# Clearing one table row later, reordering the first transfers and preparing fewer weight pieces in the first attention of an attention and FNet kernel

## The chip, the cores and the metric

The kernel runs on one core of one Trainium2 chip. The metric is the device time of that core in microseconds (us), as the median of several executions. In the text PE is TensorE, DVE is VectorE, ACT is ScalarE, POOL is GpSimd, and SP is SyncE, whose queue issues nearly all transfers (DMA). The granted clock is the share of TensorE's full clock that the profiler records as allowed: in the changed kernel the S matmuls of a tile took 0.70 us at 1.00 (at 167.63 us) and 1.14 at 0.50 (at 178.10). I call 0.50 the half clock.

## The reference

```python
# q, k, v: (8 batches, 8 heads, 576 positions, 64), float32
# attention inside chunks of 64 positions
s = scale * q_c @ k_c.T;  p = softmax(s);  x = p @ v_c      # -> (8, 576, 512)
# FNet block, per batch
u  = x + Re(FFT over channels(FFT over positions(x)))
un = (u - mean) / sqrt(var + 1e-6)
out = u + relu(un @ w_ch1) @ w_ch2         # 512 -> 2048 -> 512
```

The two weights come in as float64. The kernel turns them into float32 on the chip.

## The kernel before

A tile is two chunks of 64 positions with all heads, and 36 tiles make the eight batches. Tiles 0 to 4 are batch 0 (tile 0 also holds a chunk of batch 1). The attention of a batch yields steps. For tile n these are **S** (scores), **T** of the next tile (transposes of q and k), **V** of the tile before (P·V), and **P** (transpose of the exponentials). Batch 0 has 20 steps, 0 to 19.

```python
def att_T(n):                                   # cut
    pt = turn(lambda j: a[:, 2 * j:2 * j + 2, :].rearrange("p h d -> p (h d)"))   # PE transposes
    nc.scalar.copy(t[:, :, CH:0:-1] if low else t[:, :, 0:CH], ...)
    if low:
        nc.gpsimd.tensor_copy(t[:, :, 0:1], t[:, :, CH:CH + 1])    # GpSimd's query copy
    ...                                         # the same for k, its copy on VectorE

def load_tables():                              # start: sequence tables (cut)
    nc.sync.dma_start(out=cd, in_=dim_tab[:, 0:2, 0:HM + 1])
    nc.sync.dma_start(out=cs[:, HM + 1:DM], in_=dim_tab[:, 2, 1:HM])
    nc.sync.dma_start(out=sd, in_=dim_tab[:, 3, 1:HM])
    nc.gpsimd.memset(cs[:, 0:HM + 1], 0.0)
    nc.sync.dma_start(out=cs[0:1, 0:HM + 1], in_=dim_tab[0:1, 2, 0:HM + 1])
    nc.gpsimd.memset(cs[0:1, HM + 1:DM], 0.0)   # waits for the transfer into cs

def round_weight(i):                            # one round: front half of piece i, back half of i-1
    nc.vector.tensor_scalar(wi, hi, 0x000FFFFF, ...)          # VectorE
    nc.scalar.activation(out=w, ...)                          # ScalarE, three times (cut)
    nc.vector.tensor_scalar(p, hi, 0x7FF00000, ...)           # VectorE
    nc.vector.scalar_tensor_tensor(w, lo, ...)                # VectorE, of piece i-1
    nc.vector.scalar_tensor_tensor(p, hi, ...)                # VectorE
    nc.gpsimd.tensor_tensor(out=w, in0=w, in1=p, op=ALU.mult) # GpSimd
    load_weight(max(raws, default=i - 1) + 1)   # a freed buffer fetches the next piece, 512 KB

def shift(b):    # after V(2): one row each of the low tiles goes to the next tile
    ...          # gather by DMA into "first", then scatter by DMA back, on SP's queue
```

After the shift, the fold adds and subtracts low and high tiles on VectorE and gives `pm`. The Fourier stage is two sets of matmuls, z (over positions, from `pm`) and mix (over channels). Then follow the norms and the MLP in groups of tiles, with matmuls up and dn. In group 0 of the MLP one or two rounds are issued per step until all 33 are done. The attention of batch 1 starts between the dn matmuls of that group:

```python
t0 = KF + 1 if cur == 0 else ...                # KF = 16 steps of "up" first
```

The start of the driver issues the transfers, and the loop of batch 0 has the rounds at steps 4, 7, 10, 13, 16 and 19:

```python
for n in range(first[1]):                       # q, k of tiles 0 to 4, v of 0 to 2,
    load(n)                                     # three weight pieces after tile 1,
    ...                                         # the tables after tile 2 (cut)
for i in range(3, len(RAWS)):
    load_weight(i)
for step, _ in enumerate(attention(0)):
    if step == 9:
        turn_tables()
    if step > 3 and step % 3 == 1:
        round_next()
for step, _ in enumerate(fourier(0)):
    if step < 4:
        round_next()
    ...
```

## Time and profile before

| | before |
|---|---|
| median of 3 executions | 1332.5 us (1331.69 to 1332.6) |
| span in the profile | 1332.0 us (that execution took 1333.76) |
| PE busy | 1265.9 us, 95% |
| S of tile 1 starts | 29.14 us |
| gather of the shift issued | 53.97 us |
| z runs without a gap from | 62.83 us |
| MLP starts (first up matmul) | 97.63 us |
| dn of group 0 starts | 166.56 us |
| first S of batch 1 | 173.52 us |
| up of group 1 starts | 265.11 us |

The lower rows are read from the timeline. They are the landmarks by which two kernels are compared. Before the change 36 of PE's 66 us of idle time lie in the first 63 us and another 17 between there and dn. From 265 us on it is busy for 1058.9 of 1067 us, so a microsecond saved early should reach the end unless something in between eats it.

The view of waits sums, for PE in the first 60 us, what ended its idle time. Its columns are the total in us, how often, and the longest. The row at its top is the one that the change is aimed at:

```profile
PE sc L269 <- POOL qT L254: 14.6, 1, 14.6
```

### The profile page before, as it was taken

What the parts mean: (1) busy time and instruction counts of PE and PEld (TensorE: products, weight loads), DVE (VectorE), ACT (ScalarE), POOL (GpSimd) and SP (SyncE); (2) the same over time, 40 slices, a digit from 0 to 9 for tenths busy, and PEclk for the clock granted to TensorE, in tenths of its full rate; (3) what the DMA queues carried; (4) which work ended last, traced back from release to release, by engine and by line L of the source; (5) the groups of instructions that cost most, each with busy time, mean ns of one, the idle gap of its engine ahead of it and who ended that gap; (6) DMA issues with size and microseconds to landing.
All of it is one profiled execution on the core that took longest, in us unless ns stands there. A gap on an engine that the chain in (4) does not pass through costs nothing.

```text
span 1332.0 us, 13660 instructions
## 1 busy us (share of the span) xinstructions
PE 1265.9 (95%) x5616; PEld 611.1 (46%) x5616; DVE 345.4 (26%) x649; ACT 253.4 (19%) x517; POOL 124.9 (9%) x186
## 2 busy tenths in 40 slices
PE   3679798999999999999999999999999999999998
PEld 2434354544444445544444445444444444444443
DVE  1868951511132104210322033211411130001000
ACT  1537720122011201121112111210111001100100
POOL 0214402101100201002100210020002010000000
PEclk9669998999999999999999999999999999999999
DMA  9734431122012101211021002210100000000000
GB/s 194 170 91 142 142 73 41 25 56 48 16 32 51 37 7 26 57 31 33 16 56 40 17 15 48 50 41 8 32 17 1 8 16 8 0 16 16 0 8 24
DMA packets 126260, 56.99 MB, mean 43 GB/s; under 512 B 116533, under 2 KB 117046, under 8 KB 126198
## 3 DMA queue, kind: packets, MB, share of 16 engines
q1 hardware_dynamic: 124598, 55.73, 17.0%
q8 instruction: 44, 0.72, 0.2%
q10 hardware_dynamic: 1600, 0.39, 0.2%
q14 instruction: 18, 0.15, 0.0%
HBM read 46.50 MB, written 9.44 MB: 42 GB/s over the span
## 4 chain that ended last, share of the span: by engine, by line
PE 88%; DVE 5%; DMA 2%; SPq 2%; ACT 1%; issue 1%; POOL 1%; DVEq 0%; ACTq 0%; POOLq 0%
PE dn L553 37%; PE up L541 34%; PE z L418 5%; PE pt L242 4%; PE mix L461 4%; PE sc L269 1%; PE xp L307 1%; PE z L428 1%; DVE power L223 1%; DMA xall<-in_moe_w_ch_dram 1%; SPq L156 1%; DVE power L231 1%; DVE w L221 1%; DVE w L230 1%; DVE unT L510 1%
## 5 line engine op out<-in xcount | busy, mean ns | idle before, releaser
L541 PE MATMUL up<-unT,w 128*128 128x512 f32 x1152 | 518.2, 601 | 9.1 <-ACT h L548 8.2
L553 PE MATMUL dn<-w,h 128*128 128x512 f32 x1152 | 517.5, 599 | 0.0
L541 PEld LDWEIGHTS up<-unT,w 128*128 128x128 f32 x1152 | 213.8, 191 | 255.9 <-issue 239.7
L553 PEld LDWEIGHTS dn<-w,h 128*128 128x128 f32 x1152 | 213.5, 191 | 246.0 <-issue 243.6
L548 ACT ACTIVATE h<-up 128x512 f32<-128x512 f32 x144 | 85.7, 595 | 427.1 <-PE up L541 427.0
L572 DVE TENSOR_TENSOR o<-dn,xall 128x512 f32<-128x512 f32 x36 | 24.8, 690 | 248.6 <-PE dn L553 248.6
L278 DVE TENSOR_REDUCE mx<-sc 128x8 f32<-128x512 f32 x36 | 24.8, 690 | 221.8 <-PE sc L269 221.8
L316 DVE TENSOR_TENSOR xall<-xp,rd 128x512 f32<-128x512 f32 x36 | 24.8, 689 | 127.0 <-PE xp L307 127.0
L232 POOL TENSOR_TENSOR w<-w,power 128x512 f32<-128x512 f32 x32 | 43.4, 1357 | 88.9 <-DVE power L231 88.9
L418 PE MATMUL z<-tk,pm 128*128 128x289 f32 x128 | 42.5, 456 | 7.2 <-POOL pm L362 4.0
L476 POOL TENSOR_TENSOR xall<-y,xall 128x513 f32<-128x513 f32 x14 | 24.2, 1727 | 258.7 <-DVE y L469 258.7
L286 ACT ACTIVATE ex<-ex 128x512 f32<-128x512 f32 x36 | 22.6, 629 | 107.1 <-DVE ex L280 107.1
L269 PE MATMUL sc<-kT,qT 64*64 64x64 f32 x1152 | 26.8, 235 | 16.1 <-POOL qT L254 14.6
L436 ACT COPY zf<-z 128x256 f32<-128x256 f32 x32 | 11.9, 372 | 149.1 <-PE z L418 103.8
L269 PEld LDWEIGHTS sc<-kT,qT 64*64 64x64 f32 x1152 | 21.7, 143 | 37.7 <-issue 21.9
L418 PEld LDWEIGHTS z<-tk,pm 128*128 128x128 f32 x128 | 25.7, 208 | 27.9 <-issue 16.3
L259 DVE COPY kT<-pt 128x512 f32<-128x512 f32 x36 | 24.5, 681 | 48.1 <-PE pt L242 48.1
L307 PEld LDWEIGHTS xp<-v,pT 64*64 64x64 f32 x1152 | 21.2, 141 | 26.7 <-issue 22.2
L512 ACT COPY unT<-pt 128x512 f32<-128x512 f32 x18 | 10.5, 584 | 111.6 <-PE pt L242 111.6
L254 POOL COPY qT<-qT 128x8 f32<-128x8 f32 x16 | 3.2, 199 | 300.9 <-ACT qT L252 300.9
L288 DVE TENSOR_REDUCE rd<-ex 128x8 f32<-128x512 f32 x36 | 24.7, 686 | 25.8 <-ACT ex L286 25.8
L242 PEld LDWEIGHTS pt<-ident,un 128*128 128x128 f32 x144 | 18.6, 147 | 25.8 <-issue 22.2
(87 smaller groups left out, 762.7 us busy)
## 6 DMA issues: line engine op xcount, KB each, us to landing
xall<-in_moe_w_ch_dram SPq DMA_DIRECT2D x32, 512.0 KB
v<-in_v_dram SPq DMA_DIRECT2D x142, 64.0 KB
q<-in_q_dram SPq DMA_DIRECT2D x34, 128.0 KB
k<-in_k_dram SPq DMA_DIRECT2D x34, 128.0 KB
out_dram<-o SPq DMA_DIRECT2D x16, 256.0 KB
out_dram<-o SPq DMA_DIRECT2D x32, 128.0 KB
q<-in_q_dram SPq DMA_DIRECT2D x14, 256.0 KB
k<-in_k_dram SPq DMA_DIRECT2D x14, 256.0 KB
```

Of the source, the lines that this page charges most:

```text
L232: nc.gpsimd.tensor_tensor(out=w, in0=w, in1=p.bitcast(FP32), op=ALU.mult)
L242: nc.tensor.transpose(pt[:, j, :], src(j), ident)
L269: nc.tensor.matmul(out=sc[t0:t0 + CH, e, j * CH:(j + 1) * CH], lhsT=a[r0:r0 + D, 2 * j + c, 0:CH], rhs=b[r0:r0 + D, j, t0:t0 + CH], start= ...
L278: nc.vector.tensor_reduce(out=mx, in_=s4, axis=AX.X, op=ALU.max)
L307: nc.tensor.matmul(out=xp[t0:t0 + CH, e, j * D:(j + 1) * D], lhsT=a[r0:r0 + CH, j, t0:t0 + CH], rhs=b[r0:r0 + CH, c, j, :], start=True, st ...
L316: nc.vector.tensor_tensor(out=xo.rearrange("p (j e d) -> p e j d", j=NJ, e=2), in0=xp[:, :, 0:NJ * D].rearrange("p e (j d) -> p e j d", j=NJ),
L418: nc.tensor.matmul(out=z[:, 0:NQ], lhsT=pm[p, fold_, half], rhs=tk[p, i, fold_, :], start=(i == 0), stop=(i == NM), skip_group_check=(T == 2),
L461: nc.tensor.matmul(out=o[:, cols], lhsT=zt[:, T], rhs=tab, start=(T == 0), stop=(T == 3), skip_group_check=True,)
L541: nc.tensor.matmul(out=up[:, 0:cols], lhsT=w1[:, kk, m * 128:(m + 1) * 128], rhs=unT[:, kk, 0:cols], start=(kk == 0), stop=(kk == KD - 1),)
L548: nc.scalar.activation(out=h1[:, m, 0:cols], in_=up[:, 0:cols], func=ACTF.Relu)
L553: nc.tensor.matmul(out=dn, lhsT=h1[:, m, s * 128:(s + 1) * 128], rhs=w2[:, m, :], start=(m == 0), stop=(m == KF - 1),)
L572: nc.vector.tensor_tensor(out=o, in0=dn, in1=natural(n), op=ALU.add)
```

## The change

The change takes the clearing of one row of the table `cs` off the way of GpSimd's query copy. It orders the first transfers by when they are needed. It does three of six rounds later, outside the attention, and it puts the addition of high tiles (the HI add) on GpSimd for batch 0 too.

```diff
@@ load_tables
             nc.sync.dma_start(out=t[r0 + 1:r0 + CH, NM], in_=seq_tab[1:CH, NM])
+
+    def load_dim_tables():
         nc.sync.dma_start(out=cd, in_=dim_tab[:, 0:2, 0:HM + 1])
         ...
         nc.sync.dma_start(out=cs[0:1, 0:HM + 1], in_=dim_tab[0:1, 2, 0:HM + 1])
-        nc.gpsimd.memset(cs[0:1, HM + 1:DM], 0.0)
@@ turn_tables, called at step 9
         nc.scalar.copy(a[:, :, NL + 1:NQ], b[:, :, NL + 1:NQ])
+        nc.gpsimd.memset(cs[0:1, HM + 1:DM], 0.0)
@@ fourier
-                eng = nc.gpsimd if kind(n) == HI and b > 0 else nc.vector
+                eng = nc.gpsimd if kind(n) == HI else nc.vector
@@ driver
-        for n in range(first[1]):
+        for n in range(3):
             load(n)
-            if n < 3:
-                load_v(n)
-            if n == 1:
-                for i in range(3):
-                    load_weight(i)
-            if n == 2:
-                load_tables()
-        for i in range(3, len(RAWS)):
+            load_v(n)
+        load(3)
+        load_tables()
+        load_weight(0)
+        load(4)
+        load_weight(1)
+        load_dim_tables()
+        for i in range(2, len(RAWS)):
             load_weight(i)
@@ attention of batch 0
-            if step > 3 and step % 3 == 1:
+            if step > 7 and step % 4 == 1:
                 round_next()
```

The last line makes the steps 9, 13 and 17. In the changed kernel the line numbers are two higher (L269 becomes L271, and so on).

## The prediction

> **What bounds the kernel now.** I read the page first, then the waits and the timeline of the first 210 us, the DMA view of the first 40 us, and the busy time by stretch. The page's slices are 33.3 us each.
>
> ```profile
> PE   3679798999999999999999999999999999999998
> ...
> PEclk9669998999999999999999999999999999999999
> DMA  9734431122012101211021002210100000000000
> ```
>
> TensorE (PE) is the bound from the fourth slice on. The change acts on the first five: the first batch's attention and Fourier stage, while there is no other batch to fill PE. Of 66 us in which PE is idle (1332.0 span less 1265.9 busy), most lies there. The largest single idle time is 14.62 us:
>
> ```profile
> 28.64 0.30 POOL L179 MEMSET cs<- 1x255 f32 x1 [27.08 <-DMA cs<-in_dim_tab_dram]
> 28.89 0.19 POOL L254 COPY qT<-qT 128x8 f32<-128x8 f32 x1
> ...
> 29.14 1.13 PE L269 MATMUL sc<-kT,qT 64*64 64x64 f32 x32 [14.62 <-POOL qT L254]
> ```
>
> GpSimd (POOL) stands at the clearing of one row of cs until a table transfer lands; the small copy of tile 1's queries is behind it, and PE behind that copy. The data of tile 1 had long been there. But DMA is at nine tenths or more in this slice too (0.90 to 1.00 in each 10 us up to 40, by the busy times of stretches). The DMA view of 0 to 40 us, one column per us:
>
> ```profile
> GB/s 0 0 142 194 195 164 186 215 216 182 151 235 205 328 397 355 293 171 99 113 103 213 222 194 147 235 310 226 155 178 181 180 197 199 281 341 330 150 27 14
> DMA packets 16599, 7.72 MB, mean 193 GB/s; under 512 B 15061, under 2 KB 15574, under 8 KB 16598
> ```
>
> q, k and v come in 256 B packets at 180 to 200 GB/s (columns 3 to 7 and 29 to 33), the weight pieces (4 KB packets) at 330 to 400. All that is issued ahead of the loop lands by about 37 us.
>
> The end of the first attention is not bound by PE either:
>
> ```profile
> 53.97 1.22 SPq L334 DMA_DIRECT2D first<-xall  x2
> ...
> 57.16 1.14 PE L307 MATMUL xp<-v,pT 64*64 64x64 f32 x32 [2.35 <-ACT pT L297]
> ...
> 58.05 0.69 DVE L351 TENSOR_TENSOR sum<-xall 128x512 f32<-128x512 f32 x1 [1.31 <-DMA xall<-first]
> ...
> 62.83 1.33 PE L418 MATMUL z<-tk,pm 128*128 128x289 f32 x2 [1.71 <-DVE pm L362]
> ```
>
> The rows' shift (L334, the transfer queue SP issues it) is a gather and a scatter by DMA; the fold waits for it, and the Fourier matmuls for the fold. PE runs densely from 62.83.
>
> Then the first MLP group, where 23 of the 33 rounds of weight preparation are done:
>
> ```profile
> 97.60:166.60 69.00, 60.74 (x129) 25.71 (x130) 61.36 (x85) 48.74 (x78) 29.07 (x21) 0.94 0.42 137
> ```
>
> Columns: stretch, length, busy us of PE, PE loads, VectorE (DVE), ScalarE (ACT), POOL. DVE is the bound there (61.4 of 69): 128 up matmuls at 0.43 us would be 55 us, and PE waits 8.2 us for h, which queues on ACT between the rounds.
>
> **What the Trainium skill says.** "TensorE: Matmul & The Clock Gate", table at its head: VectorE, ScalarE and GpSimdE have strict first-in first-out queues. The trace agrees: a ready 0.19 us copy stood 14 us behind a memset. "GPSIMD Engine Reference", Engine selection: two-input elementwise work is about twice as slow there as on VectorE. The trace: the HI add takes 1.727 us on POOL and 0.66 us on DVE, 2.6 times. "DMA: Bandwidth & Descriptors", Specifications: line rate wants 512 B or more. Agrees: 187 GB/s in 2 to 10 us, all 256 B, against 330 to 400 for weights. The first page, Part 1, says about 3.4 us of sustained work releases the half clock. The trace differs: the z matmuls are back to back from 62.8 to 82.5 and that stretch's mean granted clock is 0.50.
>
> **The change part by part.**
>
> *Clearing the row later.* The copy follows its query copy, so tile 1's scores start when kT is out, at 13.95 + 0.64 = 14.6 instead of 29.1. That is 14.5 us for PE, at first. New bound: transfers.
>
> *Order of transfers.* In MB: q, k, v of tiles 0 to 2 2.36; q, k of 3 0.52; sequence table 0.89; w0 0.52; q, k of 4 0.52; w1 0.52; dimension tables 0.53; w2 to w4 1.57. Tiles 0 to 2 at 187 GB/s take 12.6 us and land at some 15 us, in time. Tile 4's q and k land near 26, needed near 27. The total, 7.4 MB, is the same, so all of it still lands at 36 to 37. Behind it, in SP's order and ahead of the gather, are v3 0.26, q5 k5 0.52, v4 0.26, q6 k6 0.52, v5 0.26. Before, v3 landed at 38 and two weight pieces (w5, w6) stood among the rest; now there are none. 1.57 MB at 185 GB/s is 8.5 us: v5 lands at 36.5..38 + 8.5 = 45 to 46.5. Before, the gather was issued 1.5 us ahead of v5's landing (53.97), so now at 43.7 to 45: earlier by 9 to 10, not 14.5. So transfers cut the 14.5 us by a third.
>
> *Fewer pieces.* Rounds at attention steps 9, 13, 17 instead of 4, 7, 10, 13, 16, 19. A round costs DVE 0.42 + 0.42 + 0.68 + 0.68 = 2.2 us and ACT 0.63 + 0.71 + 0.72 = 2.06. Three fewer would spare 6.6 us of DVE, but attention now waits for DMA, so this hides nothing more. And step 17 is a bad place: it comes after the folds, which wait for the shift, and ahead of tile 4's pT copy. That copy on ACT then waits for the fold, L221 0.42, ACT's three 2.06; then follow pT 0.58, V matmuls 1.1, the product 0.7, POOL 0.3, sum 0.7, pm 0.4: z about 6.4 us after the last fold (60.67 before), where it was 62.83 - 60.67 = 2.2. That gives back 4.2. z starts densely at about 44.4 + (60.67 - 53.97) + 6.4 = 57.5, or 57 if DMA has fewer holes: 5.5 us earlier.
>
> *HI add on POOL.* y is ready, DVE does LO's add 0.69 and statistics 0.69 + 0.18, POOL the HI add 1.5 to 1.7 meanwhile. DVE's 0.66 goes, a wait of 0.2 to 0.3 comes: 0.4 us, twice: 0.8. The MLP starts 6.3 us earlier, at 91.3.
>
> *The three rounds that moved.* In the MLP they run at (170.6 - 97.4) / 23 = 3.18 us each, 3.05 without the slow start: 9.2 us more of DVE. Up's pace, 1.5 rounds a step, does not change. But the last two are issued after h of m = 15, ahead of batch 1's scores:
>
> ```profile
> 170.68 1.26 POOL L232 TENSOR_TENSOR w<-w,power 128x512 f32<-128x512 f32 x1 [0.63 <-DVE power L231]
> ...
> 174.28 0.69 DVE L278 TENSOR_REDUCE mx<-sc 128x8 f32<-128x512 f32 x1 [3.68 <-PE sc L269]
> ...
> 178.51 0.60 PE L242 MATMUL pt<-ident,ex 128*128 128x128 f32 x4
> 179.04 0.69 PE L269 MATMUL sc<-kT,qT 64*64 64x64 f32 x32
> ```
>
> DVE has 3.68 us of slack at mx; 9.2 more makes it late by 5.5. PE has dn matmuls until 178.5, 1.4 us after what P needs. I expect P and the next scores 3.4 to 4.9 us later: 4 us lost. w2's last pieces come in time (needed some 85 us after the MLP's start, done at 83).
>
> Sum: 5.5 + 0.8 - 4 = 2.3 us off 1332.5, so 1330. The two losses (step 17 and DVE's lateness) are derived from program order and could be smaller; DMA could also have fewer holes than before (99 to 113 GB/s at 18 to 20 us). I put 1328.
>
> **Rivals.** (a) The wait goes and nothing takes its place: 14.5 + 6.6 + 0.8 = 22 us, 1310. For it: the wait is single and large. Against it: DMA's nine tenths in the first slice. (b) Clock: a denser attention keeps PE at full clock and z's 19.7 us at 0.50 become some 12: 8 us below the figure above, 1320. Against it: PE still has to wait for the shift right ahead of z. (c) The moved rounds cost their whole 9.2 us, or a pause in dn lets the clock fall: 9.2 - 4 = 5.2 us worse than the sum, 1335.5. For it: DVE is the bound in that stage.
>
> **Range and chances.** 1316 to 1336 holds half of (b), and nearly all of (c). Faster by 2% needs 26.6 us, more than (a): 0.02. Slower by 2%: 0.01. Within: 0.97.
>
> **What would show it.** Right: no wait of PE for the query copy; tile 1's scores near 14.7 us; DMA at 9 tenths without a gap to some 45 us; the gather at 44 to 45; the fold's wait for the scatter longer than 1.31; round 2 between fold and V of tile 4; z dense from 57; the MLP from 91; mx of batch 1 late, PE idle 3 to 5 us before its P. Wrong if the gather comes well before 43, if z starts before 54, or if dn shows no new idle time. After that stage all should be equal, shifted.

## The result

| | before | changed |
|---|---|---|
| median | 1332.1 us (1329.53 to 1332.6, 4 executions) | 1335.12 us (1334.33 to 1335.66, 4 executions) |
| span in the profile | 1332.0 | 1332.5 |
| S of tile 1 | 29.14 | 14.72 |
| gather issued | 53.97 | 46.37 |
| last fold operation ahead of tile 4's product ends | 60.67 | 52.69 |
| z without a gap from | 62.83 | 59.44 |
| MLP | 97.63 | 93.57 |
| dn of group 0 | 166.56 | 160.67 |
| first S of batch 1 | 173.52 | 167.63 |
| second S of batch 1 | 179.04 | 178.10 |
| up of group 1 | 265.11 | 265.63 |

The ratio is 1.0026, with a 95% interval of 1.0009 to 1.0043. Here and below a ratio is the mean time of one kernel's fast executions over the mean of the other's in the same rounds of timing, so it is not quite the ratio of the medians quoted. The change lies within 2%. A second timing of the changed kernel, on another chip, gave 1.0010 (0.9998 to 1.0022). So no gain is shown. The change probably costs a few us: 3.5 and 1.3 by the two ratios, 3.0 and 2.3 by the medians; only the first interval excludes zero. The two profiled spans differ by only 0.5 us. The profiled execution of before was slower than its median (1333.76 against 1332.1) and that of the changed kernel a little faster (1334.33 against 1335.12), so the two profiles explain where time was moved but understate the loss.

The page of the changed kernel, in its 40 slices of 33.3 us (tenths of busy time, granted clock, DMA's share):

```profile
PE   5479888999999999999999999999999999999998
...
PEclk8569988999999999999999999999999999999999
DMA  9625431022012101211021002210100000000000
```

The first slice of PE went from 3 to 5, the second from 6 to 4. The wait has moved one slice to the right. DMA's first digit is still 9, and the sixth slice (167 to 200 us) fell from 9 to 8 for PE and to 8 for the clock.

The waits of PE in the first 60 us (total, times, longest):

```profile
PE xp L309 <- ACT pT L299: 10.4, 1, 10.4
PE pt L244 <- DMA start<-in_q_dram: 6.8, 1, 6.8
PE pt L244 <- DMA q<-in_q_dram: 6.1, 1, 6.1
PE pt L244 <- DMA cs<-in_dim_tab_dram: 3.3, 1, 3.3
```

The row for the query copy is gone. In its place stand waits for transfers of 6.1 and 3.3 us, and a new largest one: 10.4 us in front of V of tile 4. (The profile puts the 3.3 us down to a transfer into `cs`. What these transposes read is tile 4's q, and in e2 the same wait is booked to q.) The timeline of the changed kernel shows what holds the gather. Its columns are start, length, engine, operation, and in brackets the idle time before it and what ended that:

```profile
14.72 1.14 PE L271 MATMUL sc<-kT,qT 64*64 64x64 f32 x32 [0.22 <-DVE kT L261]
...
32.66 0.69 DVE L318 TENSOR_TENSOR xall<-xp,rd 128x512 f32<-128x512 f32 x1 [0.40 <-PE xp L309]
...
35.56 2.98 SPq L146 DMA_DIRECT2D k<-in_k_dram  x1
...
40.81 1.09 PE L244 MATMUL pt<-ident,q 128*128 128x128 f32 x4 [6.11 <-DMA q<-in_q_dram]
```

Tile 1's scores start 14.42 us earlier, as intended. But SP spends 2.98 us on the issue of one k transfer, while the weight pieces and tables issued ahead of it drain (the last piece lands at 38.13). From 31.52 to 46.37 us SP does nothing but issue seven groups of q, k and v (2.59, 1.36, 2.98, 2.69, 0.60, 0.58 and 3.56 us, together 14.36 of 14.85), and the gather is next in that queue. What it copies was ready long before: tile 2's product (L318) ends at 33.35 us, 13.0 us ahead of the gather. In the kernel before, that product ended at 48.69, 5.3 us ahead. So the data came 15.34 us earlier, and the gather only 7.60.

The timeline around the shift and the round of step 17:

```profile
46.37 1.21 SPq L336 DMA_DIRECT2D first<-xall  x2
...
50.47 0.69 DVE L353 TENSOR_TENSOR sum<-xall 128x512 f32<-128x512 f32 x1 [5.57 <-DMA xall<-first]
...
52.62 0.41 DVE L223 TENSOR_SCALAR w<-xall 128x512 uint32<-128x512 uint32 x1
...
54.96 0.57 ACT L299 COPY pT<-pt 128x512 f32<-128x512 f32 x1
...
55.58 1.13 PE L309 MATMUL xp<-v,pT 64*64 64x64 f32 x32 [10.40 <-ACT pT L299]
...
59.44 1.33 PE L420 MATMUL z<-tk,pm 128*128 128x289 f32 x2 [1.46 <-DVE pm L364]
```

DVE waits 5.57 us for the scatter and folds. Then it begins the round (52.62), on whose ACT instructions tile 4's pT copy has to wait in ACT's queue. That copy runs at 54.96. P·V of tile 4, the product, the last fold and z are behind it. The gather came 7.60 us earlier than before, z only 3.39.

The second place is the start of batch 1 in the first MLP group, in the same view:

```profile
172.50 1.75 DVE L233 SCALAR_TENSOR_TENSOR power<-xall,power 128x512 uint32<-128x512 uint32 x1
174.17 0.68 DVE L280 TENSOR_REDUCE mx<-sc 128x8 f32<-128x512 f32 x1
...
176.76 1.12 PE L244 MATMUL pt<-ident,ex 128*128 128x128 f32 x4 [3.98 <-ACT qT L254]
...
178.10 1.14 PE L271 MATMUL sc<-kT,qT 64*64 64x64 f32 x32 [0.22 <-DVE kT L261]
```

The scores had been ready since about 168.3 us, but DVE was still on the rounds that the change had moved here. PE stands still for 3.98 us. Before, there was no such pause. The stretch view (length, busy us of PE, PE loads, DVE, ACT, POOL, then the granted clock, DMA's share, GB/s) shows what followed in the changed kernel:

```profile
172.80:182.00 9.20, 5.02 (x46) 4.01 (x47) 6.34 (x10) 2.79 (x5) 2.36 (x3) 0.63 0.07 15
```

and in the kernel before:

```profile
172.80:182.00 9.20, 9.20 (x98) 5.50 (x97) 4.47 (x9) 2.44 (x5) 0.20 (x1) 1.00 0.27 60
```

In half-microsecond stretches the clock of the changed kernel is 0.50 from 175.1 to 182.0 us. Before, it was 1.00 all through here.

The balance by landmarks: at the MLP's start the changed kernel is 97.63 − 93.57 = 4.06 us ahead. The up stage is another 1.83 us shorter (67.10 against 68.93): the half clock that z leaves behind ends 3.1 us after its start and not 5.4, which is worth some 1.2 us, and PE's wait for h fell from 8.2 to 7.5 us. So it is 5.89 us ahead at dn. At up of group 1 it is 0.52 us behind, so 6.41 us were lost in between: 3.98 us of pause and 2.43 us beside it. PE worked from 176.76 to 182.0 at half clock, 5.24 us, half of which is 2.6, which is about that remainder.

### The profile page after: what moved, and what is told of

Same layout as the page of the kernel before. It is cut to its first block, busy times and chain, and to the rows that moved or that the text cites. A ratio compares the mean times of both kernels' runs of the same rounds, so it can differ in the third digit from the quotient of the medians.

```text
span 1332.5 us, 13664 instructions
## 1 busy us (share of the span) xinstructions
PE 1266.8 (95%) x5616; PEld 612.4 (46%) x5616; DVE 346.8 (26%) x647; ACT 254.1 (19%) x517; POOL 130.6 (10%) x188
## 4 chain that ended last, share of the span: by engine, by line
PE 87%; DVE 6%; DMA 3%; SPq 2%; ACT 0%; issue 0%; POOL 0%; DVEq 0%; POOLq 0%
PE dn L555 37%; PE up L543 34%; PE z L420 5%; PE pt L244 4%; PE mix L463 4%; PE sc L271 1%; PE xp L309 1%; DVE power L225 1%; DMA xall<-in_moe_w_ch_dram 1%; PE z L430 1%; DVE power L233 1%; DVE w L232 1%; DVE w L223 1%; SPq L156 1%; SPq L146 1%; DVE unT L512 1%
## 5 line engine op out<-in xcount | busy, mean ns | idle before, releaser
L318 DVE TENSOR_TENSOR xall<-xp,rd 128x512 f32<-128x512 f32 x36 | 24.9, 690 | 129.8 <-PE xp L309 129.8
L478 POOL TENSOR_TENSOR xall<-y,xall 128x513 f32<-128x513 f32 x16 | 27.5, 1721 | 264.0 <-DVE y L471 264.0
L438 ACT COPY zf<-z 128x256 f32<-128x256 f32 x32 | 11.9, 372 | 155.7 <-PE z L420 110.4
L420 PEld LDWEIGHTS z<-tk,pm 128*128 128x128 f32 x128 | 25.7, 208 | 26.1 <-issue 14.6
L309 PE MATMUL xp<-v,pT 64*64 64x64 f32 x1152 | 26.5, 233 | 11.1 <-ACT pT L299 11.1
L271 PEld LDWEIGHTS sc<-kT,qT 64*64 64x64 f32 x1152 | 21.8, 143 | 24.3 <-issue 23.1
L244 PEld LDWEIGHTS pt<-ident,un 128*128 128x128 f32 x144 | 18.6, 147 | 24.9 <-issue 21.7
```

Source lines behind the costliest of these rows:

```text
L244: nc.tensor.transpose(pt[:, j, :], src(j), ident)
L271: nc.tensor.matmul(out=sc[t0:t0 + CH, e, j * CH:(j + 1) * CH], lhsT=a[r0:r0 + D, 2 * j + c, 0:CH], rhs=b[r0:r0 + D, j, t0:t0 + CH], start= ...
L309: nc.tensor.matmul(out=xp[t0:t0 + CH, e, j * D:(j + 1) * D], lhsT=a[r0:r0 + CH, j, t0:t0 + CH], rhs=b[r0:r0 + CH, c, j, :], start=True, st ...
L318: nc.vector.tensor_tensor(out=xo.rearrange("p (j e d) -> p e j d", j=NJ, e=2), in0=xp[:, :, 0:NJ * D].rearrange("p e (j d) -> p e j d", j=NJ),
L420: nc.tensor.matmul(out=z[:, 0:NQ], lhsT=pm[p, fold_, half], rhs=tk[p, i, fold_, :], start=(i == 0), stop=(i == NM), skip_group_check=(T == 2),
L478: eng.tensor_tensor(out=x[:, 0:w], in0=y[:, 0:w], in1=x[:, 0:w], op=ALU.add)
```

## The experiments

My theory after reading the traces: the wait that was removed had hidden a limit in the transfers, the round of step 17 cost the first batch 4 to 5 us, and the three rounds that moved cost a pause with a fall of the clock. Rivals were that the HI add or the order itself was harmful, that the pause costs nothing because DVE's work has to be done anyway, and that the memset was never worth more than it gave. Ratios are against the kernel before, in the same rounds.

| run | median us | ratio (95%) | gather | z | MLP | up of group 1 |
|---|---|---|---|---|---|---|
| before | 1332.1 | | 53.97 | 62.83 | 97.63 | 265.11 |
| changed | 1335.12 | 1.0026 (1.0009, 1.0043) | 46.37 | 59.44 | 93.57 | 265.63 |
| e1_memset_only | 1329.84 | 0.9989 (0.9976, 1.0002) | 51.26 | 60.15 | 95.35 | 261.19 |
| e2_round_19 | 1329.97 | 0.9981 (0.9969, 0.9993) | 45.07 | 53.56 | 87.64 | 260.02 |
| e3_rounds_fourier | 1328.06 | 0.9968 (0.9956, 0.9980) | 45.46 | 53.95 | 91.66 | 259.57 |
| e4_old_rounds | 1327.69 | 0.9966 (0.9954, 0.9978) | 49.94 | 58.82 | 91.01 | 257.04 |
| e5_hi_vector | 1329.63 | 0.9965 (0.9949, 0.9980) | 50.84 | 59.73 | 93.99 | 260.98 |
| e6_shift_first | 1320.90 | 0.9908 (0.9895, 0.9920) | 33.04 | 43.82 | 78.77 | 252.93 |
| e7_side_later | 1317.27 | 0.9879 (0.9864, 0.9895) | 32.98 | 43.31 | 78.67 | 250.18 |
| e8_four_rounds | 1321.56 | 0.9912 (0.9899, 0.9924) | 32.64 | 49.61 | 84.73 | 253.20 |
| e9_side_two_later | 1322.23 | 0.9926 (0.9914, 0.9938) | 33.24 | 44.40 | 77.83 | 253.46 |
| e10_weights_behind | 1325.34 | 0.9940 (0.9927, 0.9952) | 40.02 | 48.55 | 82.47 | 257.77 |
| e11_changed_again | 1334.67 | 1.0010 (0.9998, 1.0022) | 46.57 | 59.65 | 93.59 | 266.00 |
| e12_clearing_back | 1339.99 | 1.0055 (1.0042, 1.0068) | 50.79 | 65.43 | 97.69 | 271.05 |

All outputs are right. e1 to e4 ran on one chip, e5 to e8 on a second, e9 to e11 on a third, e12 on a fourth, each with its own runs of before (medians 1332.19, 1333.47, 1332.40, 1332.32).

**e1_memset_only**: the kernel before, with the clearing moved and nothing else.

```diff
@@ load_tables
-        nc.gpsimd.memset(cs[0:1, HM + 1:DM], 0.0)
@@ turn_tables
+        nc.gpsimd.memset(cs[0:1, HM + 1:DM], 0.0)
```

> The kernel before with the clearing of the cs row moved and nothing else. My theory (transfers bound the stage; the three moved weight pieces and the round behind the folds are losses): tile 1's scores start near 14.7 us, but the gather still comes only behind the transfers ahead of it, at 48.5 to 50 (before 53.97, changed kernel 46.37); V of tile 4 does not wait for a round behind the folds; z dense at 58 to 59, the MLP at 93 to 94, ten rounds done by then, no pause of PE at batch 1's first P; 4 us faster than before, ratio 0.997. Rival (the queue of GpSimd was the bound of the stage): 14 us faster, ratio 0.989. Second rival (the new order of transfers is what brings the MLP forward): no gain, MLP at 97.

Tile 1's scores start at 14.63 us, 14.51 earlier, but the gather came only 2.71 us earlier and z 2.68. The span fell by 3.9 us and the median by 2.4. In PE's waits of its first 62 us the query copy's 14.6 us are gone, but the waits for q transfers grew from 6.8 to 16.1 us, and z waits 7.0 us for the fold. The gather was 1.3 us later than I expected. So removing the wait by itself is worth about a fifth of its length (2.7 of 14.6 us) at the gather. What reaches the end is not clear of noise: the interval of the ratio, 0.9976 to 1.0002, just includes no gain at all.

**e2_round_19**: the changed kernel with the third round of the attention at its very end.

```diff
-            if step > 7 and step % 4 == 1:
+            if step in (9, 13, 19):
```

> The changed kernel with its third round at attention step 19 (after the last fold) instead of 17. My theory: V of tile 4 no longer waits 10.4 us for pT, z dense at 54.5 to 55.5 instead of 59.4, the MLP at 89 to 90 instead of 93.6; the pause of 4 us in the first dn tile stays, so 4 us faster than the changed kernel: some 1331, ratio to before 0.9990. Rival (the place does not matter, since z waits for the shift anyway): z at 59, ratio as that of the changed kernel, 1.0026.

```profile
45.05 1.13 PE L309 MATMUL xp<-v,pT 64*64 64x64 f32 x32 [0.73 <-ACT pT L299]
...
53.56 1.33 PE L420 MATMUL z<-tk,pm 128*128 128x289 f32 x2 [1.70 <-DVE pm L364]
```

The timeline shows P·V of tile 4 after a wait of 0.73 us in place of 10.40. The path from gather to z is 53.56 − 45.07 = 8.49 us, where the changed kernel has 59.44 − 46.37 = 13.07: the place of this one round cost 4.58 us there. The other 1.30 of z's 5.88 us are the earlier gather. The span is 5.5 us shorter and the pause before P of tile 5 is still 3.96 us. So what z gained reached the end nearly in full, and the pause is another matter.

**e3_rounds_fourier**: e2, with the three missing rounds added to the Fourier steps, ahead of the MLP.

```diff
         for step, _ in enumerate(fourier(0)):
             if step < 4:
                 round_next()
+                if step < 3:
+                    round_next()
```

> As the run before it, and three more rounds in the first batch's Fourier steps (two in each of steps 0 to 2), so that ten rounds are done when the MLP starts, as in the kernel before. My theory: the pause of PE in the first dn tile and the half clock after it go (worth 6 us), against 0 to 2 us of waits for zf copies: the MLP at 89 to 91, 1324 to 1326, ratio 0.994 to 0.9955. Rival (the pause comes from weights' transfers, which were put back in order, or from the clock, not from the number of rounds left): the pause stays at about 4 us and the time at that of the run before it.

There is no pause in dn, as expected. But the mix matmuls now wait 1.19 us for a VectorE operation on z (into `zr`) and 3.74 us for ACT's copy of z, which stand behind the rounds, and the MLP starts 4.02 us later than in e2. At up of group 1 the two differ by 0.45 us, at the end by 1.9 in the medians with intervals that overlap. The MLP's start and the median both missed what I expected (89 to 91 us and 1324 to 1326). The three rounds cost about 4 us in either place.

**e4_old_rounds**: the changed kernel with the six rounds where they were before.

```diff
-            if step > 7 and step % 4 == 1:
+            if step > 3 and step % 3 == 1:
```

> The changed kernel with the old places of rounds in attention (steps 4, 7, 10, 13, 16, 19). My theory: rounds 0 and 1 now wait for w0 and w1 (landing 23 to 28 us) ahead of attention's own work, which is hidden behind the transfers; two more weight pieces stand ahead of the gather, so it comes at 49 to 50; no round behind the folds, z dense near 58.5, the MLP at 92 to 93, no pause in the first dn tile: 1327, ratio 0.9965. Rival (fewer pieces are a gain, as the change means): 3 to 6 us slower than the changed kernel, 1338 to 1341.

The pause is gone and the kernel is faster than the changed one, by 8.6 us in the spans and 7.4 in the medians (of different chips). The gather comes at 49.94, 4.87 later than in e2: each finished round frees a buffer and so fetches a 512 KB piece, and two such pieces stand in SP's queue among v3, k5, v4, q6 and v5. PE also waits 8.94 us in front of tile 3's transposes, as the second round waits for its weight. On the other hand the clock went to 1.00 at 70.8 us, inside z, and z to the end of mix is 18.71 us against 22.53 in e2. (In e5, with the same rounds, the clock was not freed inside z and this took 21.87 us, so it is not the rounds' doing.) So doing fewer rounds in the attention does bring the gather forward, by about the time of two pieces, and it costs that much or more later.

**e5_hi_vector**: e4 with the HI add back on VectorE. That is e1 plus the new order of transfers.

```diff
-                eng = nc.gpsimd if kind(n) == HI else nc.vector
+                eng = nc.gpsimd if kind(n) == HI and b > 0 else nc.vector
```

> The changed kernel with the old places of rounds (as the fourth run) and, besides, the HI add of the first batch back on VectorE. So it differs from the first run only in the order of transfers, and from the fourth only in the engine of two adds. My theory: 0.8 us slower than the fourth run (its MLP started at 91.0, of which 0.8 is given back): 1328.5; and 1.4 us faster than the first run, which is the worth of the order. Rival (the adds on GpSimd cost, since they take 1.68 us instead of 0.66): 1 to 2 us faster than the fourth run.

The spans of e1 and e5 are 1328.1 and 1327.9 us, and the ratios overlap, as do those of e4 and e5. Neither the order alone nor the HI add can be told from nothing in the time. The local effect of the HI add is visible in this pair: from the start of the first LO add to the end of the last operation on `rstd`, the chain takes 8.51 us in e4 and 9.38 in e5, so 0.87 us (8.50 in the changed kernel, 9.37 in the one before). This run does not show that it reaches the end.

**e6_shift_first**: a test of the transfer limit. Of the transfers only those that the first batch needs and weight pieces 0 and 1 stand ahead of the shift; pieces 2 to 4, the dimension tables, and q, k, v of batch 1 follow it. Among the first ones the sequence table now comes after tile 4's q and k.

```diff
+    def after_shift():
+        for i in range(2, len(RAWS)):
+            load_weight(i)
+        load(first[1]); load_dim_tables(); load_v(first[1]); load(first[1] + 1)
@@ attention: called once ready(2) has issued the shift; T(5) is left to Fourier step 3
+                if n + 2 == first[1]:
+                    after_shift()
@@ driver: rounds at 9, 13, 19; turn_tables at 14; the clearing at Fourier step 1
```

> The changed kernel with the first batch's shift ahead of what does not concern it: ahead of the gather stand only q, k, v of tiles 0 to 4, the sequence table, w0 and w1 (5.9 MB instead of 9.3); w2 to w4, tile 5, the dimension tables and tile 6 follow the scatter; tile 5's transposes move into the Fourier stage, the third round to step 19, the clearing of the row into the Fourier stage. My theory (what stands ahead of the gather in the queue sets the end of the first attention): gather at 31 to 33 (46.4 in the changed kernel), z dense at 39 to 43 (59.4), the MLP at 73 to 77 (93.6), the pause of PE in the first dn tile still there at about 4 us: 1314 to 1320, ratio 0.986 to 0.991. Rival (the stage is bound by VectorE and ScalarE, not by transfers): z not before 50, ratio 0.996 or more.

```profile
33.04 1.21 SPq L335 DMA_DIRECT2D first<-xall  x2
...
43.82 1.33 PE L429 MATMUL z<-tk,pm 128*128 128x289 f32 x2 [1.78 <-DVE pm L363]
```

The gather is 12.03 us earlier than in e2 and z 9.74. In the median 9.1 us of it arrive. z and the MLP still came 0.8 and 1.8 us after the ranges that I expected. That settles the first part of the theory: what held the gather was the queue of transfers in front of it. Tile 2's product ends at 30.95 us here, and the gather follows 2.1 us behind it, not 13.0. How z's gain divides is not settled, since e6 also takes tile 5's transposes out of PE's attention. With them out of the way the gather is 20.93 us earlier than before, more than the length of the removed wait, and 12.6 us of it reach the end in the median (1333.47 to 1320.90).

**e7_side_later**: e6, with batch 1's attention one step later in the first MLP group, to give DVE time to finish the rounds.

```diff
-                    t0 = KF + 1 if cur == 0 else ...
+                    t0 = KF + 2 if cur == 0 else ...
```

> As e6_shift_first, and batch 1's attention starts one step later in the first MLP group, so that its scores come after VectorE's last rounds. My theory (VectorE's lateness makes the pause): the pause before batch 1's first P shrinks from 4 to 0 to 2 us and the half clock after it goes, 3 to 6 us faster than e6_shift_first. Rival (the pause is moved to w2's last pieces or to batch 1's Fourier stage, which now has a step less): within 1 us of e6_shift_first, with the idle time at dn or at z of batch 1.

This is the fastest version, 1317.27 us, 1.2% below before. But my reason for it failed: the pause stayed, at 3.99 us. What changed is the order after it. In e6's timeline:

```profile
163.24 1.11 PE L243 MATMUL pt<-ident,ex 128*128 128x128 f32 x4 [3.96 <-ACT qT L253]
164.57 1.13 PE L270 MATMUL sc<-kT,qT 64*64 64x64 f32 x32 [0.22 <-DVE kT L260]
```

and in e7's:

```profile
162.94 1.11 PE L243 MATMUL pt<-ident,ex 128*128 128x128 f32 x4 [3.99 <-ACT qT L253]
163.85 4.68 PE L564 MATMUL dn<-w,h 128*128 128x512 f32 x8
```

In e6 scores with a small gap follow the pause, in e7 a block of eight dn matmuls. The clock is at 0.50 for 6.83 us in e6 (162.69 to 169.52) and for 3.41 us in e7 (162.60 to 166.01). That is 3.4 us less of half clock, worth about 1.7 us. PE's wait at z of batch 1 also fell, from 3.80 to 2.28 us. Together that is 3.2 us, where dn's start to up of group 1 shrank by 2.42 (105.76 to 103.34) and the medians by 3.6. That the order of the work is what lets the clock recover sooner is my reading of this pair; no run tested it alone. There is a rival: in all fourteen kept traces the granted clock changes on a grid of 3.41 us, so the two runs differ by one step of it. Where on the grid PE resumes (0.55 us after the fall of the clock in e6, 0.34 in e7) may have decided, and not the order. The gain was in the range that I expected, though the reason for it had failed: that is luck.

**e8_four_rounds**: e6 with a fourth round in the attention, at step 16.

```diff
-            if step in (9, 13, 19):
+            if step in (9, 13, 16, 19):
```

> As e6_shift_first with a fourth round in attention, at step 16 (behind tile 4's scores). My theory: one round less after the MLP's start takes 3 us of VectorE's lateness: the pause falls from 4 to 1 us, against up to 2 us that the round adds ahead of tile 4's product: 1 to 3 us faster than e6_shift_first. Rival: the round stands in the chain as the one at step 17 did, z 2 to 4 us later, no gain.

The pause shrank to 0.83 us, and the clock stayed at 1.00 there. But P·V of tile 4 waits 7.1 us for ACT's pT copy, z comes 5.79 us later than in e6, and the ratio is the same as e6's. A round put into the path of the first batch costs what the shorter pause saves. The rival that expected no gain was right, though it had put z only 2 to 4 us later.

**e9_side_two_later**: e6 with the start two steps later.

```diff
-                    t0 = KF + 1 if cur == 0 else ...
+                    t0 = KF + 3 if cur == 0 else ...
```

> As e7_side_later, with batch 1's attention one more step later. In e7 the pause stayed at 3.99 us, because the scores moved only 3 us and VectorE is free for them only at 160.3 us after the start. Theory (the scores must come after VectorE's last round): now the scores come at 160 to 162, no idle time above 1 us before batch 1's first P, 1 to 3 us faster than e7: 1314 to 1316. Rival (batch 1 now has too few steps left, so its Fourier stage waits): the pause goes, but idle time of the same size comes at z of batch 1 or at the scores of tile 6; within 1 us of e7.

```profile
PE pt L243 <- ACT qT L253: 4.0, 4, 1.0
PE z L429 <- POOL pm L363: 3.6, 1, 3.6
PE dn L564 <- POOL w L233: 1.6, 2, 0.9
```

PE's waits from 140 to 230 us show the pause in four parts of about 1 us: with fewer steps left for batch 1, a tile's S, T and P fall into one step with no dn matmuls between them. The dn matmuls themselves wait for the last weights, and z waits 3.6 us. Up of group 1 comes 3.28 us later than in e7, and the ratio is 0.0047 worse. The expected gain was missed.

**e10_weights_behind**: e2, with only weight pieces 2 to 4 and the dimension tables moved behind the shift (and the clearing, which needs these tables, in the Fourier stage).

```diff
@@ attention, after the shift of batch 0
+                if n + 2 == first[1]:
+                    load_dim_tables()
+                    for i in range(2, len(RAWS)):
+                        load_weight(i)
@@ driver
-        load_dim_tables()
-        for i in range(2, len(RAWS)):
-            load_weight(i)
```

> e2_round_19 with only w2 to w4 and the dimension tables behind the scatter instead of ahead of the loop (2.1 MB less ahead of the gather, with nothing else moved but the clearing of the row, into the Fourier stage). At 340 GB/s for weights and some 250 for tables that is 6.5 us. Theory (transfers ahead of the gather set the end of the first attention): gather at 38 to 39.5 instead of 45.1, z dense at 46.5 to 48 instead of 53.6, the MLP at 80.5 to 82.5 instead of 87.6, the pause in dn unchanged: 5 to 7 us faster than e2_round_19, ratio to before 0.993 to 0.9945. Rival (VectorE, ScalarE or the scatter's own latency binds): gather earlier but z not before 51, ratio 0.997 or more.

The gather is at 40.02, 5.05 us earlier than in e2 and short of what I expected; z is 5.01 earlier, and up of group 1 by 2.25. The ratio falls from 0.9981 to 0.9940. So 2.1 MB of weights and tables were a little under half of e6's 12 us, and the remainder lies in the rest of e6's edits. That it is above all batch 1's q, k and v behind the shift is likely, but no run tested it alone.

**e11_changed_again**: the changed kernel itself, on another chip.

> The changed kernel once more, beside the kernel before on the chip of these runs. The interval of the first comparison, 1.0009 to 1.0043, should hold again: the median 2 to 4 us above that of before; the pause before batch 1's first P at about 4 us again. If it comes out equal or faster, the small loss was of that chip.

The times are those of the result above to within 0.2 us at the gather and 0.4 us in the span. The loss is smaller here, and its interval (0.9998 to 1.0022) just reaches zero. That the changed kernel is no faster than before holds on both chips; how much slower it is stays within a few us.

**e12_clearing_back**: the changed kernel with the clearing back where it was.

```diff
@@ load_dim_tables
+        nc.gpsimd.memset(cs[0:1, HM + 1:DM], 0.0)
@@ turn_tables
-        nc.gpsimd.memset(cs[0:1, HM + 1:DM], 0.0)
```

> The changed kernel with the clearing of the row put back ahead of the query copy, all else as changed. The dimension tables now land later than before (32.3 us in the changed kernel, 28.6 in the one before), so GpSimd would stand there until 32.6. Theory: tile 1's scores at 32.9 instead of 14.7; the chain of 15 to 16 us from there to V of tile 2 then ends behind the transfers, gather at 48 to 50 instead of 46.4, tile 3's product and the folds at 54 to 56, z dense at 63 to 66 instead of 59.4, some 5 us slower than the changed kernel: 1337 to 1342, ratio 1.004 to 1.007. Rival (18 us of wait come back whole): 1350, ratio 1.014. Second rival (transfers hide the wait altogether): as the changed kernel.

```profile
32.18 0.30 POOL L181 MEMSET cs<- 1x255 f32 x1 [30.62 <-DMA cs<-in_dim_tab_dram]
...
32.68 1.13 PE L271 MATMUL sc<-kT,qT 64*64 64x64 f32 x32 [17.91 <-POOL qT L256]
```

With the tables later in the order, the wait grows to 17.91 us. Yet the gather moves by only 4.42 us, z by 5.99, and the spans by 5.5: from a wait of 17.91 us the clearing's move is worth about 5.5 in the spans (4.7 to 5.4 by the medians, each taken over its own before), just as e1 got 3.9 in the spans and 2.4 in the medians out of 14.6.

## Why the prediction was right or wrong

The class and the range were right: I gave 0.97 to within 2% and 1316 to 1336 us, and it came to 1335.12, inside by 0.9 us. The direction was wrong. I put the point at 1328, 4 us faster, and the change is a few us slower. That the figure of rival (c), 1335.5, lies so near is luck: it put 5.2 us on dn alone, where 2.4 came. Step by step:

- **"That is 14.5 us for PE, at first."** Right: 14.42 (14.72 against 29.14). e1 and e12 show that the wait itself was never worth that, as the text said of transfers. The next statement, that tile 4's q and k land near 26 and are needed near 27, was off: PE wanted them at 25.2 and waited 3.29 us, until 28.50.
- **"1.57 MB at 185 GB/s is 8.5 us ... so now at 43.7 to 45".** This is the first step that failed in size. The gather came at 46.37, 2.0 us behind the middle that I used (44.4). From 36 to 47 us DMA moved only 152 GB/s at a share of 0.77. I took bytes over a rate, and my own sign for it, DMA at nine tenths without a gap to some 45 us, did not come: from 38 to 39 us its share was 0.20, while SP issued without a pause. So this queue seems paced by SP's issues, of which one k transfer took 2.98 us and v5 3.56; that is read from one trace, and no run tested it. That transfers in front of the gather hold it was right, and e10 and e6 confirm it by moving the gather to 40.02 and 33.04.
- **"step 17 is a bad place ... That gives back 4.2."** Right: z came 6.75 us after the last fold operation ahead of tile 4 (59.44 − 52.69), where the text had 6.4, and gather to z grew from 8.86 to 13.07 us, by 4.21. e2 takes 4.58 of it back. The text's "this hides nothing more" about the three fewer rounds is right only beside the sentence on w5 and w6: without those two pieces the gather is 4.87 us earlier (e4 against e2).
- **"z starts densely at about ... 57.5"** came to 59.44, all of it from the gather.
- **"HI add ... 0.8."** In size right (9.38 us in e5 to 8.51 in e4, 0.87); no run shows that it reaches the end.
- **"The MLP starts 6.3 us earlier, at 91.3."** It started at 93.57, 4.06 earlier, mostly the gather again. The statement that up's pace does not change held for the rounds, but not for PE: with an earlier full clock and shorter waits for h, up was 1.83 us shorter.
- **"I expect P and the next scores 3.4 to 4.9 us later: 4 us lost."** This is the second step that failed in size. The pause measured 3.98 us, and mx ran late behind the rounds as described, but the loss from dn to group 1 was 6.41 us. The rest is the half clock after the pause. Rival (c) named it ("a pause in dn lets the clock fall"), and I left it out of the sum although the pause that I expected was as long as it turned out.
- **The last step, "so 1330 ... I put 1328".** It moved the point in the wrong direction. The reasons given, losses "could be smaller" and "DMA could also have fewer holes", both went the other way.

In spans the sum of the prediction was −6.3 + 4 = −2.3. What the traces show is −4.06 − 1.83 + 6.41 = +0.52. The terms missed are +2.24 at the MLP's start, −1.83 in up and +2.41 in dn. The medians differ by 3.02, so a further 2.5 us between spans and medians is the scatter of single executions, which I can't assign to a stage.

Of the rivals, (a) is refuted by e1: the wait goes and only a part of it arrives (2.7 us at the gather; 3.9 in the span, 2.4 in the median). (b) did not occur in the changed kernel. In e2 the mean clock from z to the end of mix was 0.56, although PE was busy there for 22.49 of 22.50 us. But in four of the fourteen kept traces (e3, e4, e9 and e12) the clock was freed inside z, each time 11.9 to 12.1 us after its start. These are just the four in which a step of the 3.41 us grid falls there; in the other ten no step lies between 11.8 and 12.8 us, and the clock stayed at 0.50 for 18.6 us or more. So it looks as if the place of z on this grid decides, and not how dense the attention was; no run set it on purpose. It also means that a single trace's times after z contain some luck.

Where the gain went can be told in one line: 14.42 us at tile 1 became 7.60 at the gather (transfers), 3.39 at z (the round of step 17), 5.89 at dn (HI add, an earlier full clock, shorter waits for h), and −0.52 at group 1 (the pause, and the half clock after it).

## What to carry to other kernels

A long wait that is removed is worth only the distance to the next limit: before estimating it, list what stands ahead of the next needed transfer in its issue queue, in bytes and in issues, for that queue was the limit here, and moving what isn't yet needed behind it gained 9 us (e6 over e2), where the removal alone gained 2 to 4, hardly clear of noise. Work that is put off lands somewhere: move it only to a stage whose engines have slack, and not between an operation that waits and the copy that the next matmuls need on an in-order engine. A pause of TensorE of some 4 us cost more than itself, by the half clock after it, so count it at more than its length.

## What the Trainium skill lacked or had wrong

- "TensorE: Matmul & The Clock Gate", Part 1, puts the release of the half clock at about 3.4 us of sustained work. After the pauses that was about right: the half clock lasted 3.41 us in e7, and 6.83 in e6 and the changed kernel, one and two steps of the grid of 3.41 us. In z it was not: in the kernel before the clock stood at 0.50 for the whole of some 19.7 us of back-to-back matmuls, and in e4 it was freed 12 us after z's start. For matmuls that are no transposes I found no way on the page to tell which work counts as sustained.
- "GPSIMD Engine Reference", Engine selection, says about twice as slow for two inputs. The HI add took 1.68 to 1.73 us on GpSimd against 0.66 on VectorE, about 2.6 times.
- "DMA: Bandwidth & Descriptors" tells how bandwidth depends on the size of rows, but I found nothing there on how long an issue holds the issuing queue when large transfers are ahead of it: 0.60 us for one issue of q at 41.38 us, 1.36 for the same form behind the weights at 34.16, 2.98 for k next to it, and 14.36 of 14.85 us of SP spent on issues ahead of the gather.
- No page that I read says what an early wait in an in-order engine is worth to the whole program. Here it was, in the spans, 3.9 us out of a wait of 14.6 (e1), and 5.5 out of 17.9 (e12).
